# A spectral mixing and hard-swish kernel: the last four k of the first tokens computed straight from their spectrum, and two batches' stores moved between queues

## The chip, the cores and the metric

The kernel runs on one core of one Trainium2 chip. The metric is the device time of one execution, in microseconds (us), as the median of several runs. TensorE is called PE here, VectorE DVE, ScalarE ACT, GpSimd POOL and SyncE SP, as in the profile.

## The reference

The input x has 8 batches of 3008 tokens with 256 channels, in fp32. Each channel is filtered along the tokens by a real FFT, a product with a complex filter and an inverse FFT. Then every token passes through a two-layer network with a hard-swish.

```
X = np.fft.rfft(x, axis=1)
Y = X * (filt_r + 1j * filt_i)[None, :, :]
y = np.fft.irfft(Y, n=3008, axis=1)          # (8, 3008, 256)
h = y.reshape(24064, 256) @ w_in             # 256 -> 2048
g = h * np.clip(h + 3.0, 0.0, 6.0) / 6.0
out = g @ w_out                              # 2048 -> 256
```

## The kernel before, in words

**The transform.** 3008 is 47 times 64. Each batch passes five stages. Stage A multiplies by a 47-point table (`a_unit`, for batch 0 `a0_unit`, L302) and leaves 24 values of k with real and imaginary part. For batches 1 to 7 the result goes to DRAM (`z_store`, L342) and returns with k outside (`t2_load`, L350); for batch 0 it stays on chip and PE turns it (`turn`, L310). Stage B (`b_unit`, L355) multiplies each k by a 64-point table, which arrives together with that k's filter rows (`table_load`, L168, six pieces of four k). `f_unit` (L363) forms the filter products in three DVE operations for two k, and `y_unit` (L376) combines them in two more. `bi_unit` (L384) multiplies back and ACT copies the result to a tile t3 (two buffers). `g_store` (L396) writes t3 to DRAM, and `t4_load` (L415) reads it back with k on the partitions. Finally `n_unit` (L425) multiplies by the last table `wai` and writes chunks of up to five groups of 94 tokens into xn, the input of the network.

Batch 0 uses a shortcut: its `bi_unit` takes the raw products of `f_unit` (two tables `wi`), and `y_unit` is not run.

**The network.** Tokens go in blocks k of 512 (47 blocks) and the 2048 hidden units in eight parts p of 256. The main program from block 1 on is a seven-product scheme (`up_1` to `up_5`, `down`) software-pipelined by one part. Block 0 is computed in the plain form (`plain_up`, L536, and `plain_down`, L545), because the sums of the weights that the seven-product scheme needs are still being made. One pair (k, p) is called a step; block 0 is steps 0 to 7, and step 8 opens block 1.

**The weights.** The host passes 64-bit floats. DVE turns each of 16 pieces of 512 KB into fp32 (`w_conv`, L221, seven or eight operations a piece), from buffers `bits` that SP fills (`load_bits`, `w_load`). The letter string `W_AT` says which pool each piece's buffer is from: o (output tiles), g (hidden tiles) or x (tiles of the block sums xt). POOL then adds up the sums (`w_sums`, L249).

**The opening.** The program is written in order by hand under a manual schedule; each engine executes its instructions in that order. Everything ahead of step 0 is in L625 to L697: load batch 0's x into the space of the weights (`x0_load`, 32 transfers), `a0_unit` eight times with two `w_conv`, then a loop over the six table pieces c (L677) with two `b_unit` and `f_unit`, the `turn` for c+1, and `bi_unit` and `g_store` for the pair before. `t4_load` for the first 564 tokens (chunks 0 and 1) is called three times: for k 0 to 15, 16 to 19 and 20 to 23, each when its store has been issued. Then PE multiplies zeros nine times (`keep_warm(9)`), DVE converts three pieces (`convert(3, False)`), and `n_unit` is run for chunks 0 and 1 before step 0.

**The plan.** From step 0 on, `at(step, function)` puts the work of the other batches between the steps. In step s, functions listed in EARLY (matmul stages) come after the first products, the others at the end. Batch 1 has its eight `a_unit` in steps 2 to 9, each followed by `z_store`, its `t2_load` from step 10, and its `b_unit` from step 12.

**Queues.** SP issues nearly all loads and the output stores. In the opening ACT issues batch 0's `g_store` and two of the last `t4_load`; later POOL issues every `z_store` and `g_store`. A transfer's issue waits until the transfer eight places back has completed (in the instruction listing they rotate through eight completion counters); ACT and SP share one such set, and POOL has another.

```
for c in range(NT + 1):
    if c < NT:
        for i in (2 * c, 2 * c + 1):
            b_unit(0, i)
            f_unit(0, i)
    if c + 1 < NT:
        turn(c + 1)
    if c:
        bi_unit(0, 2 * c - 2)
        g_store(0, 2 * c - 2, nc.scalar)
```

Of the kernel before, what the change touches and what calls it, by code (L numbers as in the profile page):

```python
# [44 lines left out]
NBLK = B * N // BLK  # L45
NJ = 5
RING = 3 * BLK


def outer(j, h):  # L50
# [4 lines left out]
def _make_tables():  # L55
    a = np.arange(NA)
    c = np.arange(NC)
    wa = np.zeros((P, P))
    wai = np.zeros((P, HC, TOK))
    start = np.zeros((P, 2 * P))  # L60
    for h in range(2):
        for k in range(KH):
            th = 2 * np.pi * ((a * k) % NA) / NA
            for g in range(2):
                wa[h * 64:h * 64 + NA, g * 64 + k] = np.cos(th)
                wa[h * 64:h * 64 + NA, g * 64 + 32 + k] = -np.sin(th)
            start[h * 64:h * 64 + NA, P + 4 * k + h] = np.cos(th)
            start[h * 64:h * 64 + NA, P + 4 * k + 2 + h] = -np.sin(th)
    wb = np.zeros((P, KH, P))
    wi = np.zeros((P, 3, NC))  # L70
    re, im = slice(0, NC), slice(NC, P)
    for k in range(KH):
        for q in range(64):
            f, sign = (k + NA * q, 1.0) if q < 32 else (NA * (q - 31) - k, -1.0)
            th = 2 * np.pi * ((c * f) % N) / N
            cs, sn = np.cos(th), np.sin(th)
            if f in (0, NF - 1):
                sn = np.zeros(NC)
            wb[re, k, q], wb[im, k, q] = cs, sign * sn
            wb[re, k, HALF + q], wb[im, k, HALF + q] = -sn, sign * cs  # L80

    for q in range(64):
        g, sign = (q, 1.0) if q < 32 else (31 - q, -1.0)
        co, si = (f([2 * np.pi * ((j * g) % NC) / NC for j in range(HC + 1)]) for f in (np.cos, np.sin))
        ab = np.concatenate([co, np.zeros(HC - 1) if q == 63 else si[1:HC]])
        wi[q, 0], wi[HALF + q, 0] = ab, sign * ab
        wi[q, 1], wi[HALF + q, 1] = ab, -ab
        wi[q, 2], wi[HALF + q, 2] = sign * ab, sign * ab
    start[:, :P] = np.eye(P)
    for j in range(HC):  # L90
        for h in range(2):
            to = slice(h * NA, (h + 1) * NA)
            for k in range(KH):
                m = 2.0 if k else 1.0
                th = 2 * np.pi * ((a * k * NC + outer(j, h) * k) % N) / N
                cs, sn = m * np.cos(th), m * np.sin(th)
                s = -1.0 if h else 1.0
                if j:
                    wai[k, j, to], wai[32 + k, j, to] = cs, -sn
                    wai[64 + k, j, to], wai[96 + k, j, to] = -s * sn, -s * cs  # L100
                else:
                    wai[h * 64 + k, j, to], wai[h * 64 + 32 + k, j, to] = cs, -sn
    f = np.float32
    return wa.astype(f), (wai / N).astype(f), wb.astype(f), wi.astype(f), start.astype(f)


@with_exitstack
def kernel(
# [8 lines left out]
):  # L117
    nc = tc.nc

    wa_np, wai_np, wb_np, wi_np, start_np = _make_tables()  # L120
    wa_d = nc.inline_tensor(wa_np, name="wa_t").ap()
    wai_d = nc.inline_tensor(wai_np, name="wai_t").ap()
    wb_d = nc.inline_tensor(wb_np, name="wb_t").ap()
    wi_d = nc.inline_tensor(wi_np, name="wi_t").ap()
    start_d = nc.inline_tensor(start_np, name="start_t").ap()


    z_d = nc.dram_tensor("z_tmp", (B, KH, P, D), FP32, kind="Internal").ap()
    g_d = nc.dram_tensor("g_tmp", (B, NU, 2, 2, NC, D), FP32, kind="Internal").ap()

    def pool(name, bufs, **kw):
# [67 lines left out]

    W_AT = "ooggxxooxxooxxoo"

    def w_before(i):
        same = [j for j in range(i) if W_AT[j] == W_AT[i]]
# [1 line left out]

    def w_load(i, q):
        if W_AT[i] == "g":
            t = gp.tile([P, 7, 256], FP32, name="g").bitcast(I32)[:, 0:4, :].rearrange("p a n -> p (a n)")  # L210
        elif W_AT[i] == "x":
            t = xtp.tile([P, 4, 256], FP32, name="xt").bitcast(I32).rearrange("p a n -> p (a n)")
        else:
            t = op.tile([P, 1024], I32, name="bits", tag="o")
        q.dma_start(t.rearrange("p (a d) -> p a d", a=2), w_part(i)[0])
        st["bits", i] = t
# [122 lines left out]
            nc.scalar.activation(out=t[:, h, :, :].rearrange("p j d -> p (j d)"), in_=ps[h], func=AXT.Copy)  # L339
        st["t1", b, c] = t  # L340

    def z_store(b, c):  # L342
        t = st.pop(("t1", b, c))
        for g in range(2):
            for ri in range(2):
                p0 = g * 64 + ri * 32
                z = z_d[b, :, ts(ri, NC), :].rearrange("k (h j) d -> k h j d", h=2)
                nc.gpsimd.dma_start(z[:, :, ds(c * XC + 2 * g, 2), :], t[p0:p0 + KH, :, :, :])  # L348

    def t2_load(b, c):  # L350
        t = t2p.tile([P, TC, D], FP32, name="t2")
# [23 lines left out]

    def y_unit(b, i):  # L376
        s1, s2 = st["y", b, i]
        y = yp.tile([P, 2, D], FP32, name="y")
        nc.vector.tensor_tensor(out=y[0:HALF], in0=s1[0:HALF], in1=s1[HALF:P], op=ALU.subtract)
        nc.vector.tensor_tensor(out=y[HALF:P], in0=s2[0:HALF], in1=s2[HALF:P], op=ALU.add)  # L380
        st["y", b, i] = y


    def bi_unit(b, i):  # L384
        ys = [st.pop(("y", b, i + v)) for v in range(2)]
        ps = [psF.tile([P, 2, D], FP32, name="psf", tag="f") for ri in range(2)]
        for v, ri in ((0, 0), (1, 0), (0, 1), (1, 1)):

            w, y = (wi[ts(ri, 64), 0, :], ys[v][ts(ri, 64)]) if b else (wi[:, 1 + ri, :], ys[v][ri])
            nc.tensor.matmul(ps[ri][ts(v, 64)], w, y, start=True, stop=True)  # L390
        t = t3p.tile([P, 2, 2, D], FP32, name="t3")
        for ri in range(2):
            nc.scalar.activation(out=t[:, ri, :, :], in_=ps[ri], func=AXT.Copy)  # L393
        st["t3", b, i] = t

    def g_store(b, i, q=nc.gpsimd):  # L396
        t = st.pop(("t3", b, i))
        for v in range(2):
            q.dma_start(g_d[b, i + v].rearrange("ri u c d -> c (ri u) d"), t[ts(v, 64)].rearrange("p ri u d -> p (ri u) d"))

# [9 lines left out]
        b, j, n = chunks[i]  # L412
        return b * N + j * TOK, n * TOK

    def t4_load(i, k0=0, k1=KH, qs=None, more=0):  # L415
        b, j, n = chunks[i]
        n += more
        for h in range(2):
            for ri in range(2):
                p0 = h * 64 + ri * 32  # L420
                (qs or (nc.sync, nc.sync))[ri].dma_start(t4[p0 + k0:p0 + k1, ds(i % 2 * NJ, n), :].rearrange("k j d -> k (j d)"),
                                  g_d[b, k0 // 2:k1 // 2, ri, :, ds(h * HC + j, n), :].rearrange("i u j d -> i u (j d)"))


    def n_unit(i, dh):  # L425
# [9 lines left out]
            done += m  # L435
        if dh and (t + n) // BLK > t // BLK > 0:
            t_sums(t // BLK)

    def xb(k, d):
        return xn[:, d, ts(k % 3, BLK)]  # L440
# [178 lines left out]
    with tc.manual_schedule():  # L619

        st["start"] = p14p.tile([P, 2, 2, P], FP32, name="p14").rearrange("p a u m -> p (a u m)")
        nc.scalar.dma_start(st["start"][:, 0:2 * P], start_d)  # L625
        zero = rp.tile([P, 512], FP32, name="r", tag="r")
        nc.vector.memset(zero, 0.0)
        nc.vector.memset(top_c, -0x40000000)
        nc.vector.memset(half_c, 0.5)
        nc.vector.memset(x0[32:64, 0:8, :], 0.0)  # L630
        nc.gpsimd.memset(x0[32:64, 8:16, :], 0.0)
        nc.gpsimd.memset(x0[32:64, 16:HC, :], 0.0)
        loaded = done = 0

        def load_bits(most):
# [10 lines left out]
                done += 1  # L646
                load_bits(NCONV if act else 0)

        def keep_warm(n):
            ps = psU.tile([P, 512], FP32, name="al")  # L650
            for i in range(n):
                nc.tensor.matmul(ps, zero[:, P:2 * P], zero, start=True, stop=True)

        nc.scalar.activation(out=zero[:, 0:1], in_=half_c, func=AXT.Copy)
        nc.scalar.dma_start(wi, wi_d)
        keep_warm(2)
        for j in range(0, HC, 4):
            x0_load(j, 4)
            load_bits({4: 1, 12: 2}.get(j, 0))
        for c in range(FB):  # L660
            table_load(0, c)
        load_bits(3)
        for j in range(0, HC, 4):
            a0_unit(j)
            convert(j in (4, 12), False)
        nc.gpsimd.memset(t4, 0.0)
        for c in range(FB, NT):
            table_load(0, c)
            if c == 3:
                load_bits(4)  # L670
        load_bits(5)
        nc.sync.dma_start(wai[:, 0:8, :], wai_d[:, 0:8, :])
        load_bits(8)
        nc.sync.dma_start(wa, wa_d)
        for i in range(2):
            w_sums(i, False)
        turn(0)  # L677
        for c in range(NT + 1):
            if c < NT:
                for i in (2 * c, 2 * c + 1):  # L680
                    b_unit(0, i)
                    f_unit(0, i)
            if c + 1 < NT:
                turn(c + 1)
            if c:
                bi_unit(0, 2 * c - 2)
                g_store(0, 2 * c - 2, nc.scalar)
            if c > 3:
                t4_load(0, (0, KH - 2 * TC, KH - TC)[c - 4], (KH - 2 * TC, KH - TC, KH)[c - 4], (nc.sync, nc.scalar)
                        if c == NT else None, 1)  # L690
        keep_warm(9)
        convert(3, False)
        for i in range(2):
            for dh in range(2):
                n_unit(i, dh)
        for i in range(2, done):
            w_sums(i, False)  # L697

# [47 lines left out]
        for n in range(1, B):  # L746
            a_at, b_at, bi_at = places(n)
            for c, s in enumerate(a_at):
                at(s, a_unit, n, c)
                at(s, z_store, n, c)  # L750
                if c >= 3:
                    at(max(a_at[c - 3], s - 6), x_load, n, c)
                elif n > 1:
# [113 lines left out]
```

## Time and profile before

| what | value |
|---|---|
| median of 3 runs | 2749.97 us (2749.27 to 2754.78) |
| profiled execution: its own time | 2751.82 us |
| profiled execution: span | 2750.0 us |
| mean granted PE clock | 0.994 |
| PE busy | 2703.0 us, 98% of the span |
| DVE busy | 1948.8 us, 71% |
| ACT busy | 1327.2 us, 48% |
| POOL busy | 398.8 us, 15% |
| moved by DMA | 194.72 MB, 71 GB/s in the mean |

The profile is of one execution, on the core's own time axis from the span's start. A row of the groups or of the timeline names the line of the code, the engine, the operation, the tiles, and in brackets what ended the idle time before it. A table by stage gives for each stretch its length, then busy time of PE, PEld (weight loads), DVE, ACT and POOL with instruction counts, the granted PE clock (1.00 is full speed), the busy share of the DMA engines and their GB/s. An fp32 matmul shows as two records, so "x4" is two instructions.

### The profile page before, as it was taken

What the parts mean: (1) busy time and instruction counts of PE and PEld (TensorE: products, weight loads), DVE (VectorE), ACT (ScalarE), POOL (GpSimd) and SP (SyncE); (2) the same over time, 40 slices, a digit from 0 to 9 for tenths busy, and PEclk for the clock granted to TensorE, in tenths of its full rate; (3) what the DMA queues carried; (4) which work ended last, traced back from release to release, by engine and by line L of the source; (5) the groups of instructions that cost most, each with busy time, mean ns of one, the idle gap of its engine ahead of it and who ended that gap; (6) DMA issues with size and microseconds to landing.
All of it is one profiled execution on the core that took longest, in us unless ns stands there. A gap on an engine that the chain in (4) does not pass through costs nothing.

```text
span 2750.0 us, 47026 instructions
## 1 busy us (share of the span) xinstructions
PE 2703.0 (98%) x18086; PEld 2404.5 (87%) x18086; DVE 1948.8 (71%) x3407; ACT 1327.2 (48%) x2658; POOL 398.8 (15%) x616
## 2 busy tenths in 40 slices
PE   8899999999999999999999999999999999999997
PEld 5477888998889988999889998899988999999997
DVE  7767856777667775678756787577775777766665
ACT  3344455444554455444554445544445444545443
POOL 1341021100211012100121001210112100100000
PEclk9899999999999999999999999999999999999999
DMA  8533233221332213321233212332123321100000
GB/s 236 154 108 89 55 89 88 67 63 41 89 90 71 58 46 88 90 73 50 54 87 94 65 48 62 87 99 69 38 57 91 92 72 38 43 23 24 19 9 16
DMA packets 119180, 194.72 MB, mean 71 GB/s; under 512 B 21981, under 2 KB 83293, under 8 KB 118829
## 3 DMA queue, kind: packets, MB, share of 16 engines
q1 hardware_dynamic: 97383, 143.89, 18.2%
q0 software_dynamic: 17728, 44.23, 7.1%
q10 hardware_dynamic: 3846, 3.60, 0.5%
q8 instruction: 143, 2.34, 0.4%
q14 instruction: 80, 0.66, 0.1%
HBM read 119.80 MB, written 71.83 MB: 70 GB/s over the span
## 4 chain that ended last, share of the span: by engine, by line
PE 94%; DVE 2%; DMA 1%; POOL 1%; issue 1%; ACT 0%; SPq 0%; POOLq 0%; DVEq 0%; ACTq 0%
PE po L529 42%; PE al L453 23%; PE be L453 17%; PE psn L428 4%; PE psf L359 3%; PE psf L336 2%; PE psf L390 2%; POOL w_all L252 0%; PE po L305 0%; PE po L359 0%; DMA xs<-in_x_dram 0%; DMA t<-g_tmp 0%; DVE g L503 0%; PE po L551 0%; POOL z_tmp L348 0%
## 5 line engine op out<-in xcount | busy, mean ns | idle before, releaser
L529 PEld LDWEIGHTS po<-w_all,g 128*128 128x128 f32 x10304 | 1368.0, 191 | 144.4 <-issue 39.2
L529 PE MATMUL po<-w_all,g 128*128 128x128 f32 x10304 | 1398.7, 276 | 5.1 <-DVE g L503 4.4
L503 DVE SCALAR_TENSOR_TENSOR g<-r,h 128x512 f32<-128x512 f32 x736 | 506.7, 688 | 270.2 <-ACT r L498 257.6
L498 ACT ACTIVATE r<-h,half_c 128x512 f32<-128x512 f32 x736 | 531.2, 722 | 331.0 <-DVE h L479 319.0
L453 PE MATMUL al<-xt,w_all 128*128 128x256 f32 x2208 | 660.1, 381 | 4.1 <-ACT s L474 2.5
L479 DVE TENSOR_TENSOR h<-be,s 128x512 f32<-128x512 f32 x368 | 254.3, 691 | 263.8 <-PE be L453 251.3
L453 PE MATMUL be<-xn,w_all 128*128 128x256 f32 x1472 | 437.8, 379 | 0.0
L453 PEld LDWEIGHTS al<-xt,w_all 128*128 128x128 f32 x2208 | 335.3, 192 | 6.1 <-issue 3.7
L453 PEld LDWEIGHTS be<-xn,w_all 128*128 128x128 f32 x1472 | 279.7, 190 | 37.9
L493 ACT ACTIVATE h<-al 128x256 f32<-128x256 f32 x368 | 141.3, 384 | 348.2 <-PE al L453 348.2
L484 DVE TENSOR_TENSOR h<-al,s 128x256 f32<-128x256 f32 x368 | 156.3, 425 | 165.0 <-PE al L453 163.5
L511 DVE TENSOR_TENSOR g<-g 128x512 f32<-128x512 f32 x368 | 255.1, 693 | 12.6
L474 ACT ACTIVATE s<-al 128x256 f32<-128x256 f32 x368 | 141.5, 384 | 199.8 <-PE al L453 199.8
L465 ACT ACTIVATE s<-be 128x256 f32<-128x256 f32 x368 | 141.3, 384 | 176.1 <-PE be L453 176.1
L453 PE MATMUL al<-xn,w_all 128*128 128x256 f32 x736 | 219.9, 381 | 0.5 <-ACT h L493 0.5
L453 PE MATMUL be<-xt,w_all 128*128 128x256 f32 x736 | 218.9, 379 | 0.0
L348 POOL DMA_DIRECT2D z_tmp<-t x224 | 130.1, 584 | 418.8 <-ACT t L339 415.9
L464 ACT ACTIVATE s<-al 128x256 f32<-128x256 f32 x368 | 141.4, 384 | 68.0 <-PE al L453 67.9
L513 DVE TENSOR_TENSOR g<-g 128x256 f32<-128x256 f32 x368 | 160.6, 436 | 12.5
L510 DVE TENSOR_TENSOR g<-g 128x256 f32<-128x256 f32 x368 | 156.8, 426 | 12.6
L453 PEld LDWEIGHTS be<-xt,w_all 128*128 128x128 f32 x736 | 139.8, 190 | 18.9
L585 POOL TENSOR_TENSOR o<-p,o 128x256 f32<-128x256 f32 x45 | 32.6, 726 | 813.4 <-ACT t L393 392.7
(117 smaller groups left out, 1869.9 us busy)
## 6 DMA issues: line engine op xcount, KB each, us to landing
t<-g_tmp SPq DMA_DIRECT2D x188, 120.0 KB
z_tmp<-t POOLq DMA_DIRECT2D x224, 96.0 KB, 3.3
t<-z_tmp SPq DMA_DIRECT2D x42, 512.0 KB
g_tmp<-t POOLq DMA_DIRECT2D x84, 256.0 KB, 3.8
out_dram<-o SPq DMA_DIRECT2D x321, 47.0 KB
xs<-in_x_dram SPq DMA_DIRECT2D x112, 128.0 KB
ft<-in_filt_r_dram SPq DMA_DIRECT2D x88, 128.0 KB
ft<-in_filt_i_dram SPq DMA_DIRECT2D x88, 128.0 KB
```

Source lines behind the costliest of these rows:

```text
L453: nc.tensor.matmul(ps, w_in[p][:, w, :], x, start=start, stop=stop, skip_group_check=True)
L464: nc.scalar.activation(out=s[:, 0, :], in_=al, func=AXT.Copy)
L465: nc.scalar.activation(out=s5, in_=be[:, 1, :], func=AXT.Copy)
L474: nc.scalar.activation(out=s[:, 1, :], in_=al, func=AXT.Copy)
L479: nc.vector.tensor_tensor(out=st["h"][0].rearrange("p (a n) -> p a n", a=2), in0=be, in1=s, op=ALU.add)
L484: nc.vector.tensor_tensor(out=st["h"][1][:, 256:512], in0=al, in1=s5, op=ALU.add)
L498: nc.scalar.activation(out=r, in_=st["h"][i], func=AXT.Relu, bias=half_c, scale=1.0 / 6.0)
L503: nc.vector.scalar_tensor_tensor(out=st["g", k, p][:, o:o + 2, :].rearrange("p a n -> p (a n)"), in0=st["r", i], scalar=1.0, in1=st["h"][i ...
L510: v.tensor_tensor(out=g[:, G1, :], in0=g[:, G3, :], in1=g[:, G22, :], op=ALU.add)
L511: v.tensor_tensor(out=g[:, G3:G2 + 1:2, :], in0=g[:, G3:G1 + 1, :], in1=g[:, G11:G11 + 1, :].broadcast_to([P, 2, 256]), op=ALU.subtract)
L513: v.tensor_tensor(out=g[:, G4, :], in0=g[:, G12, :], in1=g[:, G2, :], op=ALU.subtract)
L529: nc.tensor.matmul(st["po", k][bank][:, part, u, :], g[:, a, ts(u, P)], w_out[p][:, w, :], start=(p == 0 and n in OPENS and u == 0), stop= ...
```

## The change

In short: for batch 0 and the first 564 tokens, k 20 to 23 no longer go through `bi_unit`, DRAM, `t4_load` and `n_unit`. `y_unit` now forms the combined spectrum of units 10 and 11 (two k each), and a new function `direct` multiplies it with a new table `direct_t` (128 x 4 x 564 fp32) straight to tokens. Its sums stay in four PSUM tiles, and `n_first` adds the products of k 0 to 19 on top and copies to xn. `bi_unit(0, 10)` and its `g_store` still run, after `n_first`, for the later chunks. Batch 0's stores g leave from POOL's queue in place of ACT's, in a new DRAM layout (`g0_d`) with runs of 2 KB in place of 1 KB on the DRAM side; its `t4_load` reads that layout in runs of 1 KB. Batch 1's `z_store` go out from SP in place of POOL. `keep_warm(9)` is gone. The loads of weight pieces 2 to 7 move behind the table loads. The x loads become five calls (20 transfers) in place of eight (32), and their memsets are cut smaller, the first ones ahead of the others. `W_AT` has o in place of x for pieces 12 and 13.

```
-    W_AT = "ooggxxooxxooxxoo"
+    W_AT = "ooggxxooxxoooooo"
...
-    def z_store(b, c):
+    def z_store(b, c, q=nc.gpsimd):
...
+    def direct(i):
+        if "psn" not in st:
+            st["psn"] = {(c, dh): (psO.tile([P, 2, 2, P], FP32, name="po%d" % (2 + dh)).rearrange("p a u m -> p (a u m)")
+                                   if c else psF.tile([P, 512], FP32, name="psn", tag="f"))
+                         for c in range(2) for dh in range(2)}
+        for u in range(2):
+            k = 2 * i + u - KH + TC
+            for (c, dh), ps in st["psn"].items():
+                t, n = token(c)
+                nc.tensor.matmul(ps[:, 0:n], st["y", 0, i][:, u, ts(dh, P)], st["direct"][k][:, ds(t, n)],
+                                 start=k == 0, stop=False, skip_group_check=True)
+
+    def n_first():
+        for (c, dh), ps in st.pop("psn").items():
+            b, j, n = chunks[c]
+            for q in range(n):
+                nc.tensor.matmul(ps[:, ts(q, TOK)], t4[:, j + q, ts(dh, P)], wai[:, j + q, :],
+                                 start=False, stop=True, skip_group_check=True)
+            nc.scalar.activation(out=xn[:, dh, ds(j * TOK, n * TOK)], in_=ps[:, 0:n * TOK], func=AXT.Copy)
...
+        nc.vector.memset(x0[32:64, 0:4, :], 0.0)
+        nc.gpsimd.memset(x0[32:64, 4:8, :], 0.0)
         nc.vector.memset(zero, 0.0)
...
-        nc.vector.memset(x0[32:64, 0:8, :], 0.0)
...
-        for j in range(0, HC, 4):
-            x0_load(j, 4)
-            load_bits({4: 1, 12: 2}.get(j, 0))
+        for j, n, bits in (0, 4, 0), (4, 4, 1), (8, 8, 2), (16, 8, 0), (24, 8, 0):
+            x0_load(j, n)
+            load_bits(bits)
         for c in range(FB):
             table_load(0, c)
-        load_bits(3)
...
+        for i in range(2):
+            w_sums(i, False)
         for c in range(FB, NT):
             table_load(0, c)
-            if c == 3:
-                load_bits(4)
-        load_bits(5)
+        last = x0_at(HC * D - 2048, 3 * ND)
+        nc.sync.dma_start(last, direct_d[:, 0:3, :].rearrange("p k n -> p (k n)"))
+        load_bits(3)
+        st["direct"] = [last[:, ts(k, ND)] for k in range(3)] + [st["rest"][:, 0:ND]]
+        nc.sync.dma_start(st["direct"][3], direct_d[:, 3, :])
         nc.sync.dma_start(wai[:, 0:8, :], wai_d[:, 0:8, :])
-        load_bits(8)
-        nc.sync.dma_start(wa, wa_d)
-        for i in range(2):
-            w_sums(i, False)
+        load_bits(4)
         turn(0)
-        for c in range(NT + 1):
-            if c < NT:
-                for i in (2 * c, 2 * c + 1):
-                    b_unit(0, i)
-                    f_unit(0, i)
+        for c in range(NT):
+            for i in (2 * c, 2 * c + 1):
+                b_unit(0, i)
+                f_unit(0, i)
+                if c == NT - 1:
+                    y_unit(0, i)
             if c + 1 < NT:
                 turn(c + 1)
             if c:
                 bi_unit(0, 2 * c - 2)
-                g_store(0, 2 * c - 2, nc.scalar)
+                g_store(0, 2 * c - 2)
             if c > 3:
-                t4_load(0, (0, KH - 2 * TC, KH - TC)[c - 4], (KH - 2 * TC, KH - TC, KH)[c - 4], (nc.sync, nc.scalar)
-                        if c == NT else None, 1)
-        keep_warm(9)
+                t4_load(0, (0, KH - 2 * TC)[c - 4], (KH - 2 * TC, KH - TC)[c - 4], 1)
+            if c == 4:
+                load_bits(5)
+        direct(NU - 2)
+        direct(NU - 1)
+        load_bits(8)
+        nc.sync.dma_start(wa, wa_d)
+        n_first()
+        bi_unit(0, NU - 2)
+        g_store(0, NU - 2)
         convert(3, False)
-        for i in range(2):
-            for dh in range(2):
-                n_unit(i, dh)
...
-                at(s, z_store, n, c)
+                at(s, z_store, n, c, nc.sync if n == 1 else nc.gpsimd)
```

## The prediction

> **What bounds the kernel now.** I read the page first. PE is busy 98% of the span and carries the chain that ended last, so after the opening the kernel is a fixed string of matmuls: what the opening loses or gains is carried to the end unless something behind it waits.
>
> ```profile
> span 2750.0 us, 47026 instructions
> PE 94%; DVE 2%; DMA 1%; POOL 1%; issue 1%; ACT 0%; SPq 0%; POOLq 0%; DVEq 0%; ACTq 0%
> ```
>
> Next the table by stage over the first 105 us (length, busy time of PE, PEld, DVE, ACT, POOL, then clock, DMA share, GB/s).
>
> ```profile
> 46.00:56.00 10.00, 7.31 (x29) 4.95 (x30) 4.70 (x7) 2.54 (x5) 0.00 (x0) 0.83 0.96 295
> 61.50:69.50 8.00, 8.00 (x19) 3.34 (x18) 7.76 (x15) 1.08 (x2) 1.87 (x3) 1.00 0.61 170
> 69.50:77.00 7.50, 0.04 (x1) 0.02 (x1) 4.83 (x9) 0.00 (x0) 3.22 (x6) 0.74 0.17 50
> 77.00:88.00 11.00, 10.76 (x32) 7.48 (x33) 0.69 (x1) 2.20 (x5) 0.00 (x0) 0.56 0.21 65
> ```
>
> From 61.5 to 77.0 PE does nothing useful (8 us of zeros, then idle), and to 88 it runs at 0.56 clock. The chain between 55 and 90 us and the waits say why: a store goes to DRAM, k 20 to 23 come back, the tables follow.
>
> ```profile
> 70.53 3.62 DMA t<-g_tmp
> 74.63 2.40 DMA xs<-in_x_dram
> 77.03 4.55 PE psn L428 x20
> 82.96 3.47 PE al L540 x4
> ...
> 89.11 0.69 DVE g L503
> ```
>
> Last, SP's own waits from 30 to 60 us, and the places behind the opening where PE or SP wait.
>
> ```profile
> SPq L215 <- DMA g_tmp<-t: 4.6, 1, 4.6
> SPq L178 <- DMA g_tmp<-t: 2.0, 1, 2.0
> ```
> ```profile
> 99.27 2.73 PE L540 MATMUL al<-xn,w_all 128*128 128x512 f32 x4 [3.98 <-DVE g L503]
> 162.86 15.03 SPq L606 DMA_DIRECT2D out_dram<-o  x14
> 178.23 2.98 SPq L352 DMA_DIRECT2D t<-z_tmp  x3
> ```
> ```profile
> ACT t L339 <- DMA z_tmp<-t: 8.2, 3, 3.7
> PE al L453 <- ACT s L474: 2.5, 1, 2.5
> ```
>
> SP stood 6.6 us behind batch 0's stores, whose completion counters it shares with ACT, so the tables for k 16 to 23 came late.
>
> **The change, step by step.** My yardstick is the end of block 0's first DVE pair (L503): 89.80 us now (89.11 + 0.69). From there DVE converts two pieces and releases PE at 99.27, 9.5 us later, whatever came before.
>
> *x loads and memsets.* The third x transfer waits for a DVE memset that ends at 3.67 (1.91 + 1.76). The new one is half as long and comes first: ready at 0.92 + 0.9 = 1.8. Twelve of SP's issues go (8.56 us for 16 at L290, 0.53 each), but the bytes stay and the DMA share is near 1.0 from 8 to 26 us; the larger second chunk also leaves PE idle again (it waited 2.50 us at 13.49). Bounds on the end of the 47-point stage (26.15): 0 to 3 us earlier; I take 1.0.
>
> *Tables.* Stores on POOL no longer stand before SP's issues, and 1 MB of weight pieces moves behind the tables. DVE's waits at L371 (3.74 us for the filter rows, 1.67 behind them) go. Late next is PE: L359 comes at 36.22 and 40.85, a period of 4.65. The last pair is then at 36.2 + 3 x 4.65 = 50.2, less 1.0 is 49.2 (55.01 now). DVE starts 1.2 later, as now (56.23 - 55.01). Units 10 and 11 take 2 x 2.14, and the new `y_unit` four operations of 64x512 at 0.687 (L379): 50.4 + 4.3 + 2.75 = 57.5 (60.5 now). So the added DVE work costs 2.75 us and is paid.
>
> *direct.* 16 matmuls of two sizes. 470 columns: the 512-column pair of L540 takes 3.48 us for four (88.19 to 91.67), 0.87 each, so 0.80; eight make 6.4. 94 columns: L428 warm takes 1.09 us for five (123.14), 0.22; eight make 1.7. Half of the 8.1 us lies under unit 11's DVE work; the other half follows 57.5 or the first half (which needs a PSUM tile that unit 11's product frees at 56.1): end about 62.6. Its tables, 1.16 MB, lie behind the filter tables on SP, 4 us at the 295 GB/s of 46 to 56; with the tables through by about 45 they are in by 52. If that cover were gone, each us late is a us lost.
>
> *Round trip of k 16 to 19, now the last.* `bi_unit(8)`: 51.2 to 53.1 (1.94 at L390); ACT copies to 53.7; two stores on POOL, 0.65 each, to 55.0. Landing: 3.0 to 7.4 us, median 3.8 (L399): 58.8. Four loads at 0.78 (3.91 for five): 62.0. Before, the last was issued by 72.6 and PE was released at 77.0, 4.5 later; a nearer landing would be 2. I take 65.0, bounds 64 and 68.
>
> *n_first and step 0.* 12 matmuls at 0.22 (warm) are 2.6, `bi_unit(10)` 1.9 with ACT's copies beside it: PE starts step 0 at 69.6 (82.75 now). Then 4 x 0.87, ACT 0.69, DVE 0.69: 74.5. DVE's three conversions take 13.95 (60.52 to 74.47), now from 57.5 to 71.5; plus 1.4 gives 72.9, so PE's path is later, by 1.6 us. Yardstick: 74.5 against 89.8, **15.3 us gained**.
>
> *Weight pieces, POOL's sums.* Pieces 4 to 7 arrive by about 68, needed from 67 (piece 4, issued near 58) to 80. Pieces 12 and 13 wait for conversions two back; about one conversion (4.5 us) is left for 512 KB, 2 us at 250 GB/s. Cost nothing; without this cover at most 2 us each. Behind PE's L540 wait there is the same 4 us gap, so the half clock after it (0.63 in 100.0 to 104.6) stays.
>
> *Batch 1's z_store on SP.* 32 issues at 0.55 are 18 us on SP, 19 less on POOL (0.58 each). POOL was late behind its sums, ACT stood 8.2 us behind its stores, and PE lost 2.5 (L453): that goes. On SP each store waits for ACT, and the x loads queue behind it; an x piece is issued three steps of 8 us ahead, so I charge nothing there. But the last eight stores now stand between the 14 output stores (15.0 us) and `t2_load`: 4.4 us of issue and 2.7 of landing, where `t2_load` had been issued at 178.23 and was needed at 188.15. Loads of 512 KB need about 4 more: slack of 6 shrinks by 7.1 and by the 2.5: a wait of 1 to 4; I take 1.5. Net here +1.0.
>
> *keep_warm, and two rules.* Removing the zeros: PE was idle 7.5 us after them and ran at 0.56. The Trainium skill (TensorE: Matmul & The Clock Gate, Part 1) says that an idle window of about 3.4 us halves the clock. My gaps before step 0 are at most 2.4 us, so warm; were they above, `n_first` and step 0 double, an estimate of about +6 us. Against moving stores to POOL speaks the skill's SBUF — State Buffer, section SBUF: two separate sides: fast DVE operations lock POOL out of writing descriptors, 620 ns becoming 3100. The row: POOL's `z_store` between conversions takes 0.58 to 0.79 and L399 0.63 to 0.67. By the rule the two critical stores cost 5 us more, by the row nothing; the operations there (products from PSUM, `y_unit`) are not the fast kind, so I go by the row.
>
> **The sum.** 15.3 + 1.0 is 16.3: span 2750.0 - 16.3 = 2733.7. The profiled execution took 2751.82, 1.85 above the median; from the median 2749.97, **2733.5 us**.
>
> **Rivals.**
> - *Late landing on POOL's queue* (10%): stores at 7.4 in place of 3.8, and t3's two buffers make `bi_unit` wait for a store two back. Round trip +3.6, one such wait +3: gain about 10, 2740. For it: DMA share near 1 until 56. Against: median 3.8 elsewhere.
> - *More at the front* (10%): x arrives in larger runs 2 us sooner than I take, the last loads land in 2, and DVE's conversions become the limit (72.9 less 2): gain about 21, 2728.
> - *The direct path doesn't shorten the wait* (5%): the tables or k 16 to 19 come as late as k 20 to 23 did, say 73, in a DMA queue still full. Step 0 then starts at 77.6: gain 5, 2745.
> - *SP becomes the bound in steps 2 to 12* (3%), slower: if the 18 us of stores found no gaps and each x load and `t2_load` came later by them, the stores and 1 us of waits for ACT would give 19 against 15: 2754. It decides once more than 16 us reach PE. Against: SP is idle 14 us before the outputs, 122 to 127 and elsewhere.
>
> **Chances.** The sum as it stands, 72%, 2728 to 2739. A measurement of this kernel can tell about 0.2% (5.5 us) from no change. Faster by more 0.92, within 0.05, slower 0.03. Range 2725 to 2742.
>
> **What would show it.** PE at full clock up to step 0, which starts near 70; no SP wait for g stores between 30 and 50; L371 without the 3.7 us wait; yardstick near 74.5; no wait of ACT for z stores; a short PE wait for `t2_load` near 172. Wrong if PE idles over 4 us before `n_first`, if x or `t2_load` waits exceed 5 us, or if DVE's conversions wait for weight pieces.

## The result, and the profile after

| | before | after |
|---|---|---|
| median of the runs, us | 2750.51 (2749.27 to 2754.78, 4 runs) | 2741.52 (2739.87 to 2742.31, 4 runs) |
| profiled execution: own time, span | 2751.82, 2750.0 | 2741.89, 2740.1 |

The ratio is 0.9964, with a 95% interval of 0.9947 to 0.9981. The change takes 9.0 us off; 16.5 were forecast. In the profiled executions it is 9.9 us of span, and all that follows is read from those.

First the page of the changed kernel, the span and the chain's shares:

```profile
span 2740.1 us, 47054 instructions
PE 95%; DVE 3%; DMA 1%; issue 0%; POOL 0%; ACT 0%; SPq 0%; POOLq 0%; DVEq 0%; ACTq 0%
```

PE's share was 94% and is 95%; the shares are whole per cents, and the new `y_unit` operations are not on the chain. Then the same four stages as before (length, busy time of PE, PEld, DVE, ACT, POOL, then clock, DMA share, GB/s):

```profile
46.00:56.00 10.00, 9.30 (x44) 4.78 (x40) 9.28 (x14) 4.45 (x8) 2.26 (x4) 1.00 0.86 283
61.50:69.50 8.00, 4.70 (x21) 3.28 (x20) 7.76 (x16) 0.00 (x0) 0.00 (x0) 0.89 0.93 240
69.50:77.00 7.50, 7.50 (x33) 5.23 (x33) 3.24 (x7) 2.60 (x6) 0.43 (x1) 0.67 0.65 165
77.00:88.00 11.00, 8.67 (x29) 4.82 (x27) 8.86 (x14) 4.51 (x7) 7.28 (x14) 1.00 0.35 96
```

The 7.5 us without PE and the 8 us of zeros are gone; from 46 to 56 PE works 9.3 us of 10, where it had 7.3. But the clock is 0.67 from 69.5 to 77.0, which the forecast had at full. The chain of waits in that stretch:

```profile
56.27 0.43 POOL g_tmp L413
56.69 0.10 issue
56.79 4.47 DMA g_tmp<-t
...
62.66 5.50 DMA xt<-in_moe_w_out_dram
68.17 0.08 issue
68.25 4.55 PE psn L477 x20
...
75.10 1.91 PE al L582 x4
...
79.49 0.69 DVE g L545
```

The store of k 16 to 19 lands at 61.26, four loads go out to 62.62, and PE gets on at 68.25. (The chain names the weight piece that was issued behind the loads; what to make of that is tested below.) `n_first`'s first ten products (x20) take 4.55 us, a time that the kernel before showed at half clock. The yardstick is at 79.49 + 0.69 = 80.18.

SP's own waits from 30 to 60 us, the two longest:

```profile
SPq L439 <- DMA g_tmp<-t: 14.4, 4, 10.7
SPq L187 <- DMA w_all<-wb_t: 1.9, 2, 0.9
```

L439 is `t4_load`, which needs what was stored. No table and no weight piece stands behind a store any more. Behind the opening:

```profile
90.24 3.78 PE L582 MATMUL al<-xn,w_all 128*128 128x512 f32 x4 [4.57 <-DVE g L545]
```
```profile
153.28 11.96 SPq L648 DMA_DIRECT2D out_dram<-o  x14
165.29 5.86 SPq L359 DMA_DIRECT2D z_tmp<-t  x8
173.43 1.49 SPq L363 DMA_DIRECT2D t<-z_tmp  x3
```
```profile
ACT t L350 <- DMA z_tmp<-t: 0.7, 1, 0.7
PE al L495 <- ACT s L516: 0.5, 1, 0.5
```

PE still waits for DVE ahead of step 2. The eight z stores stand where the forecast put them, between the outputs and `t2_load`, and PE has no wait for `t2_load` at all. ACT's waits for z stores fell from 8.2 to 0.7 us and PE's wait for ACT from 2.5 to 0.5.

### The profile page after: what moved, and what is told of

Same layout as the page of the kernel before. It is cut to its first block, busy times and chain, and to the rows that moved or that the text cites. A ratio compares the mean times of both kernels' runs of the same rounds, so it can differ in the third digit from the quotient of the medians.

```text
span 2740.1 us, 47054 instructions
## 1 busy us (share of the span) xinstructions
PE 2700.9 (99%) x18100; PEld 2405.9 (88%) x18100; DVE 1950.4 (71%) x3411; ACT 1325.8 (48%) x2658; POOL 385.6 (14%) x598
## 4 chain that ended last, share of the span: by engine, by line
PE 95%; DVE 3%; DMA 1%; issue 0%; POOL 0%; ACT 0%; SPq 0%; POOLq 0%; DVEq 0%; ACTq 0%
PE po L571 42%; PE al L495 23%; PE be L495 17%; PE psn L449 4%; PE psf L370 3%; PE psf L347 2%; PE psf L403 2%; PE po L593 1%; PE po L316 1%; PE po L370 0%; PE al L582 0%; DVE g L545 0%; PE be L582 0%; DMA w_all<-in_x_dram 0%; DMA xt<-in_moe_w_out_dram 0%
## 5 line engine op out<-in xcount | busy, mean ns | idle before, releaser
L540 ACT ACTIVATE r<-h,half_c 128x512 f32<-128x512 f32 x736 | 531.0, 721 | 329.4 <-DVE h L521 317.3
L553 DVE TENSOR_TENSOR g<-g 128x512 f32<-128x512 f32 x368 | 255.1, 693 | 12.6
L359 POOL DMA_DIRECT2D z_tmp<-t x192 | 110.7, 581 | 414.9 <-ACT t L350 412.5
```

Source lines behind the costliest of these rows:

```text
L540: nc.scalar.activation(out=r, in_=st["h"][i], func=AXT.Relu, bias=half_c, scale=1.0 / 6.0)
L553: v.tensor_tensor(out=g[:, G3:G2 + 1:2, :], in0=g[:, G3:G1 + 1, :], in1=g[:, G11:G11 + 1, :].broadcast_to([P, 2, 256]), op=ALU.subtract)
```

## The experiments

Twelve kernels were run. Each starts from the changed kernel unless it says otherwise. The first two columns after the name are times in the profiled execution, the next two are differences, which do not depend on how the front of that execution went. The kernel before was timed again beside each group of kernels (e1 to e4, e5 to e8, e9 to e11, e12); its medians there were 2752.37, 2752.06, 2750.43 and 2750.54 us. So a difference of under 2 us between medians of different groups shows nothing.

| kernel | 47-point stage ends | step 0 | step 2 less stage end | span less step 2 | span | median (runs) |
|---|---|---|---|---|---|---|
| before | 26.15 | 82.75 | 73.1 | 2650.7 | 2750.0 | 2750.51 (4) |
| after | 27.55 | 75.03 | 62.7 | 2649.9 | 2740.1 | 2741.52 (4) |
| e1_memset | 25.78 | 73.10 | 62.5 | 2649.6 | 2737.9 | 2740.49 (4) |
| e2_warm | 30.54 | 75.45 | 60.2 | 2648.5 | 2739.3 | 2741.14 (4) |
| e3_late | 25.78 | 73.16 | 63.1 | 2649.5 | 2738.4 | 2741.83 (5) |
| e4_no_direct | 27.31 | 76.20 | 65.9 | 2649.7 | 2742.9 | 2744.31 (6) |
| e5_pieces | 26.39 | 73.44 | 62.3 | 2650.0 | 2738.7 | 2741.43 (5) |
| e6_act_store | 26.11 | 80.85 | 70.1 | 2648.9 | 2745.1 | 2748.60 (20) |
| e7_z_pool | 26.37 | 73.77 | 63.1 | 2650.3 | 2739.8 | 2743.20 (7) |
| e8_conv4 | 26.85 | 73.95 | 58.4 | 2651.3 | 2736.5 | 2737.94 (4) |
| e9_conv4_warm | 26.28 | 71.60 | 57.9 | 2650.4 | 2734.6 | 2736.68 (5) |
| e10_hold | 26.34 | 71.97 | 61.3 | 2649.5 | 2737.1 | 2739.87 (4) |
| e11_before_pool | 25.37 | 76.21 | 67.5 | 2652.0 | 2744.8 | 2748.66 (20) |
| e12_bits_zpool | 27.46 | 74.39 | 62.7 | 2653.5 | 2743.6 | 2745.07 (12) |

The column "span less step 2" moves by 1 to 2 us, and by 3 in e12: most of what the opening gains or loses stays to the end, as the forecast assumed. My theory after the result was that the shortfall lies in three places, the front, the landing of k 16 to 19, and the clock behind PE's gap before `n_first`. The rivals were that the stores on POOL land late, and that the edit in steps 2 to 12 cost more than 1 us.

**e1_memset: do POOL's memsets hold the x loads up?**

```
-        nc.gpsimd.memset(x0[32:64, 8:16, :], 0.0)
+        nc.vector.memset(x0[32:64, 8:16, :], 0.0)
```

> The changed kernel with one memset of x0 moved: columns 8 to 15 are cleared by DVE in place of POOL, so that POOL's memsets end near 5.2 us in place of 6.9 and the third x transfer finds its rows cleared early. If POOL's four memsets hold the x transfers up (theory 1), PE is released from its first wait at about 11.9 instead of 13.58, the gap before it is under 2 us, the 47-point stage ends near 25.3 instead of 27.55, and the span falls by about 2 us. If the bytes of x and of the first weight pieces set that time (theory 2), PE is released at 13.4 to 13.7 as before, the stage ends within 0.4 us of 27.55, and the span stays within 1 us.

PE's row in the timeline at the end of that wait:

```profile
13.20 12.58 PE L316 MATMUL po<-p,w_all 111*128 111x128 f32 x96 [2.37 <-DMA w_all<-in_x_dram]
```

PE is released at 13.20, against 13.58 in the changed kernel and 13.14 in e3_late, whose memsets are those of the changed kernel. Theory 1, 11.9, is out, though the chain of the changed kernel had led through the four memsets. The stage did end 1.8 us sooner, but so it did in e3_late: with this front unedited the stage ended at 25.8 to 27.6 in ten executions (after, e3 to e10 and e12; mean 26.6), and with the old front at 26.15 and 25.37. The forecast's 1.0 us of gain there isn't in the rows; if anything the new front is about 0.9 later, which two executions of the old one can't settle. What spreads the ends is when the x pieces land and how long half clock lasts behind the gap before the second chunk: 3.4 us of it in e1 and e3, where the 96 records take 12.6 us, 6.8 us in the changed kernel and e4, where they take 14.0.

**e2_warm: what does the half clock cost?**

```
+            if j == 8:
+                keep_warm(2, zero[:, P:2 * P], zero)
             a0_unit(j)
...
         direct(NU - 1)
+        keep_warm(3, st["direct"][0][:, 0:P], st["direct"][0][:, 0:470])
```

> The changed kernel with matmuls on spare data put into two waits of PE: two of 512 columns in the wait near 10 to 13.6 us, three of 470 columns between the direct products and n_first. If the half clock after these gaps is what made the 47-point stage and n_first longer than forecast (theory 1), the 96 products of the stage take 12.7 us or less instead of 13.97 (end near 26.2), n_first's 24 products take 2.7 instead of 5.4, step 0 starts near 71 instead of 75.1, and the span falls by 3 to 4 us. If the clock falls anyhow (theory 2), the durations stay at 13.9 and 5.4 and the span stays within 1 us. If DVE's conversions, done at 72.8, and not PE then hold the next step (theory 3), step 0 starts near 71 but the end of the first DVE pair moves from 80.2 only to about 76, and PE's release at 90.2 with it.

The stretch from `n_first` to step 0, first in the changed kernel, then in e2_warm (columns as above):

```profile
68.25:75.10 6.85, 6.85 (x33) 5.54 (x33) 4.45 (x9) 1.51 (x4) 0.00 (x0) 0.54 0.78 208
```
```profile
71.35:75.45 4.10, 4.10 (x33) 3.12 (x33) 3.96 (x9) 1.52 (x5) 0.00 (x0) 1.00 1.06 279
```

The same 33 recorded matmuls take 4.10 us at clock 1.00 and 6.85 at 0.54, so theory 1 holds for this gap: 2.75 us of PE time went there. Step 2 started 60.2 us behind the stage end in place of 62.7, so the gain was not lost to DVE, and theory 3 is out. In the front the test failed: the x pieces came late in this execution (a second wait of 3.22 us, stage end 30.54), so nothing can be read there. The median, 2741.14, shows no gain that can be told from none.

**e3_late: are the weight pieces in the way of k 16 to 19?**

```
-        load_bits(8)
-        nc.sync.dma_start(wa, wa_d)
         n_first()
         bi_unit(0, NU - 2)
         g_store(0, NU - 2)
+        load_bits(8)
+        nc.sync.dma_start(wa, wa_d)
```

> The changed kernel with weight pieces 5 to 7 and the table wa issued after n_first in the order of the program, so that on SP nothing but piece 4 and the loads of k 16 to 19 stands behind k 0 to 15. If the three 512 KB pieces issued at 62.7 to 63.7 hold up the landing of k 16 to 19 (theory 1), PE's wait before n_first of 3.3 us falls to about 0.5 to 1 and n_first starts near 65.5. If k 16 to 19 need 4.5 to 5.5 us to come down whatever stands behind them (theory 2), n_first starts at 67.5 to 68.5 as before. In both cases the pieces themselves come later: if DVE's second or third conversion then waits for them, its end moves from 72.8 to 75 or more and eats a part.

This was a poor edit: nothing in these lines makes SP wait, so SP issues the same loads in the same order, 0.04 us behind the last load of k 16 to 19. It tests neither theory and is of use only as the changed kernel run once more: gap before `n_first` 3.74 us, `n_first` to step 0 6.2 us, median 2741.83.

**e5_pieces and e10_hold: the same question put rightly**, once with the four pieces ahead of everything, once with pieces 5 to 7 and what is behind them held until `n_first` has begun.

```
-        load_bits(4)
+        load_bits(8)
         turn(0)
```

> The changed kernel with weight pieces 4 to 7 (2 MB) issued on SP right behind piece 3, near 42 us, where SP otherwise stands from 42.3 to 57.0, so that no 512 KB load is left around the loads of k 0 to 19. If those pieces hold up the landing of k 16 to 19 (theory 1), n_first starts 2 to 3 us after SP's last load instead of 5.6, PE's gap before it falls from 3.3 us to under 1.5, the clock stays full, n_first's 24 products take near 3 us instead of 5.4, and step 0 starts about 5 us sooner after the end of the direct products (5 instead of 10.1); the span falls by 3 to 5. If k 16 to 19 take 5.3 to 6 us to come down in any case (theory 2), all of that stays and the span is within 1 us of 2740.

```
+        if i == 5:
+            nc.scalar.activation(out=t.bitcast(FP32)[:, 0:1], in_=xn[:, 0, 0:1], func=AXT.Copy)
         q.dma_start(t.rearrange("p (a d) -> p a d", a=2), w_part(i)[0])
```

> The changed kernel with the load of weight piece 5 made to wait for n_first's first copy (ACT writes one column of its tile, out of n_first's output, ahead of the load), so that pieces 5 to 7, the table wa and the x pieces of batch 1 stand still on SP until n_first has begun. If PE's wait for k 16 to 19 is lengthened by what is issued behind them (theory 1), n_first starts 2 to 3 us behind SP's last load of k 16 to 19 instead of 5.3 to 6, PE's gap falls under 1 us, and the 24 products take near 3 us. If the four loads of 24 KB take that long by themselves (theory 2), n_first starts 5 us or more behind the last load as before. The pieces then come 10 us later: conversions in step 0 or PE's first x products may wait, so that the span may be longer in both cases.

PE's row at the start of `n_first`, first e5_pieces, then e10_hold:

```profile
66.38 4.51 PE L477 MATMUL psn<-wai,t 128*128 128x94 f32 x20 [2.44 <-DMA xs<-in_x_dram]
```
```profile
66.52 2.89 PE L479 MATMUL psn<-wai,t 128*128 128x94 f32 x20 [2.76 <-DMA t<-g_tmp]
```

Counted from SP's last load of k 16 to 19, PE is released after 5.6 us in the changed kernel (5.3 to 6.2 in e1, e3, e7, e8 and e12, whose loads there are the same), 5.0 in e10_hold (61.53 to 66.52) and 3.7 in e5_pieces (62.69 to 66.38). So the pieces behind the loads cost 0.3 to 1.2, and the chain's "xt" was only the transfer that ended last in the same wait. Piece 4, issued just ahead, costs about 1.3, and 3.7 us are left for the four loads themselves; each of these two rests on one execution. Neither theory holds as it was put: the landing is mostly its own, and partly piece 4. Nor was it all gain: in e5_pieces the g stores landed in a median of 5.7 us in place of 4.5 while 2 MB moved beside them, SP got its loads out later, and `n_first` began 40.0 us behind the stage end in place of 40.7. In both kernels the clock halved behind gaps of only 2.44 and 2.76 us.

**e4_no_direct, e6_act_store, e11_before_pool: which part carries the gain?** In e4 k 20 to 23 go through DRAM again, with nine products of zeros; e6 puts batch 0's stores back on ACT's queue; e11 is the kernel before with only those stores on POOL.

```
-                nc.gpsimd.dma_start(g0_d
+                nc.scalar.dma_start(g0_d
```

> The changed kernel without the direct products: k 20 to 23 of block 0 go through DRAM as in the kernel before, with nine matmuls of zeros in the wait, and all four loads precede n_unit; front, queues, layout of the scratch tensor and the later z stores stay as changed. If the direct products carry most of the gain (theory 1), step 0 starts 5 to 7 us later than 75.1 and the span is 2744 to 2748. If the tables that come earlier carry it (theory 2), step 0 starts within 2 us of 75.1 and the span stays near 2741.

> The changed kernel with batch 0's g stores on ACT's queue, as in the kernel before, all else as changed. If SP's 6.6 us behind those stores came from their queue (theory 1), SP stands again behind g stores between 40 and 57 us, piece 3 or the loads of k 0 to 15 go out 2 to 5 us later, and step 0 starts later by 1 to 4. If the order of the tables had done it, since after the change all tables are issued before the stores land (theory 2), nothing is late on SP; ACT's queue may even land the two last stores sooner than the 4.5 us on POOL, and step 0 starts 0 to 2 us sooner after the end of the direct products.

> The kernel before with one edit: batch 0's g stores on POOL's queue in place of ACT's. If that queue alone carries most of the change's gain (theory 1), SP's 6.6 us behind g stores and PE's 3.1 us for a table at 48.7 go, k 20 to 23 come 5 to 7 us sooner, and the span is 2743 to 2746 against 2750. If the gain needs the new order of the tables and the direct products (theory 2), SP then waits for something else, the last stores land later on POOL, and the span is within 2 us of 2750.

SP's waits from 30 to 60 us in e6_act_store, and PE's row at the third table pair:

```profile
SPq L189 <- DMA g_tmp<-t: 7.2, 2, 6.6
...
SPq L711 <- DMA g_tmp<-t: 1.9, 1, 1.9
SPq L187 <- DMA g_tmp<-t: 1.8, 1, 1.8
```
```profile
48.77 3.43 PE L370 MATMUL po<-t,w_all 128*128 128x256 f32 x8 [3.35 <-DMA w_all<-wb_t]
```

SP's longest wait in the same stretch in e11_before_pool, and the start of step 0 in e4_no_direct:

```profile
SPq L421 <- DMA g_tmp<-t: 10.3, 4, 6.1
```
```profile
76.20 3.68 PE L582 MATMUL al<-xn,w_all 128*128 128x512 f32 x4
```

L187, L189 and L711 are loads of tables. With the stores on ACT they stand 10.9 us behind stores that they don't need (in the traces SP's and ACT's transfers take turns on the same eight semaphores, POOL's on eight others), and PE's wait for a table, 3.10 us before, is back. In e11 only L421 (`t4_load`) still stands behind stores, the ones that it reads. Behind the stage end, step 2 comes 7.4 us later than in the changed kernel without POOL's queue (e6), 3.2 later without the direct products (e4), and 5.6 sooner than before with POOL's queue alone (e11, 67.5 against 73.1). The 5.6 of the queue alone and the 3.2 that the direct products add make 8.8 of the 10.4 us; 1.6 is left for the other edits and what the parts do together. So theory 1 of e6 and of e11 holds in the rows, by more than was expected of e6, and the direct products are the smaller part: step 0 came only 1.2 us later without them, not 5 to 7, though step 2 lost 3.2, since step 0 began at half clock (its first four records took 3.68 us for 1.98).

These sums rest on one execution of each kernel. The timed runs, each set against the kernel before in its own group, gained 9.0 us (changed kernel), 8.1 (e4), 3.5 (e6) and 1.8 (e11: 2748.66, ratio 0.9992, 0.9985 to 0.9999). They agree that the change without POOL's queue loses most of its gain. They do not tell the 0.9 us of the direct products from none, and they do not confirm 5 us for the queue alone: e11's profiled execution, 2746.63, is 2.0 us below its median, and that of the kernel before, 2751.82, is 1.3 above 2750.51. So how the gain divides between the two edits is open.

**e7_z_pool and e12_bits_zpool: what took the waits near step 10 away?** e7 puts batch 1's z stores back on POOL; e12 also puts weight pieces 12 and 13 back in the buffers `xt`.

```
-                at(s, z_store, n, c, nc.sync if n == 1 else nc.gpsimd)
+                at(s, z_store, n, c)
```
```
-    W_AT = "ooggxxooxxoooooo"
+    W_AT = "ooggxxooxxooxxoo"
```

> The changed kernel with batch 1's z stores back on POOL's queue. If SP's queue for them is worth what the forecast put there or a little more (theory 1), PE waits again 2 to 2.5 us for ACT near step 10, ACT again 8 us for its own stores, and the span is 1.5 to 2.5 us longer, all of it between step 8 and step 14. If DVE bounds these steps (theory 2), the waits show but PE's step 12 starts at the same distance behind step 2 and the span is within 0.7 us of 2740.

> The changed kernel with batch 1's z stores back on POOL's queue and, besides, weight pieces 12 and 13 back in the buffers named xt, in which POOL also forms the sums of block 1 (t_sums). If it is the pieces' buffers, and not the queue of the z stores, that took ACT's 8.2 us of waits and PE's 2.5 us away (theory 1), POOL stands 8 to 12 us before t_sums near 120 us, ACT waits again 5 to 9 us for its own z stores, PE again 2 to 2.5 us for ACT near 140 to 150, and the span is 2 to 3 us above the 2739.8 of the kernel with the z stores alone on POOL, if its opening is alike. If the buffers are not the cause (theory 2), POOL's wait may show, but ACT's and PE's waits stay away and the distance from step 2's start to the end stays at 2650.

In e7 the waits stayed away (PE's wait for ACT 0.5 us, no wait of ACT for z stores), and the distance from step 2 to the end is 2650.3 against 2649.9. In e12 they came back; POOL's, PE's and ACT's rows:

```profile
122.43 1.17 POOL L488 TENSOR_TENSOR xt<-xn 128x256 f32<-128x256 f32 x1 [11.07 <-issue]
```
```profile
150.72 0.84 PE L495 MATMUL al<-xt,w_all 128*128 128x256 f32 x2 [2.54 <-ACT s L516]
```
```profile
ACT t L350 <- DMA z_tmp<-t: 4.5, 2, 2.7
```

The kernel before has the same row on POOL, which the forecast left out; ahead of it stands DVE's last read of a weight piece in `xt`:

```profile
130.71 0.69 DVE L240 SCALAR_TENSOR_TENSOR y<-xt,y 128x512 f32<-128x512 f32 x1
131.91 0.80 POOL L446 TENSOR_TENSOR xt<-xn 128x256 f32<-128x256 f32 x1 [11.28 <-issue]
```

So theory 1 of e12 holds, with ACT's 4.5 us a little under the 5 to 9 expected: with pieces 12 and 13 in `xt`, POOL stands 11 us at `t_sums` until such a buffer is free (DVE's last read of a piece there ends at 122.29 in e12, POOL goes on at 122.43; 131.40 and 131.91 in the kernel before), its z stores queue behind that, ACT waits for them and PE for ACT. The distance to the end is 2653.5, 3.2 us more than e7: PE's wait of 2.5, with 3.4 us of half clock behind it (151.1 to 154.5). So the new letters of `W_AT` for pieces 12 and 13, which I had priced at nothing, are enough to remove these waits, and neither theory of e7 held. Given them, no gain of SP's queue for the z stores is shown: e7 is 0.4 us longer from step 2 to the end and 1.7 in the median (2743.20 against 2741.52), but the medians are from different groups, and 140 us behind step 2 (ACT's L540) e7 is 1.4 us ahead of the changed kernel. Whether SP's queue alone would have removed them too, with the old buffers, was not tried.

**e8_conv4 and e9_conv4_warm: the 10 us behind the yardstick.** DVE is idle from 72.84 until ACT's output at 77.77, and up to the yardstick but for one operation; then it converts two pieces while PE waits.

```
-        convert(3, False)
+        convert(4, False)
...
-        for i, s in enumerate((0, 0, 1, 2, 2, 3, 4, 4, 5, 5, 6)):
+        for i, s in enumerate((0, 1, 2, 2, 3, 4, 4, 5, 5, 6)):
```

> The changed kernel with one more weight piece converted ahead of step 0 (four in place of three, and one less in step 0), in the 6.6 us in which DVE stands idle from 72.8 to 79.5. If after the first pair PE waits only for DVE's two conversions (theory 1), PE is released for step 2 at 5.5 to 6 us behind the end of that pair instead of 10.1, 4.5 us sooner, PE's gap before it is under 0.5 us and no half clock follows it (2 to 3 us more); of that 3 to 7 us stay in the span if the later steps have slack on DVE. If DVE stays the bound up to step 8 (theory 2), the release comes sooner but PE waits elsewhere up to 140 us and the span falls by 0 to 2 us.

> The changed kernel with both edits that moved PE so far: four weight pieces converted ahead of step 0, and three matmuls of 470 columns of spare data between the direct products and n_first. If the two gains add (theory 1), n_first's 24 products take near 3 us, step 0 starts about 7.7 us behind the end of the direct products, step 2 starts right behind step 1, and the span is 2 to 3 us below the 2736.5 of the four conversions alone, near 2734. If DVE, which now ends its fourth conversion only at about 77.3, takes the place of PE (theory 2), step 0 starts sooner but its first DVE pair waits, step 2 starts at most 0.5 us sooner than with the four conversions alone, and the span stays within 1 us of 2736.5.

 (e9 is e8 with the second `keep_warm` of e2.)

PE's row at the start of step 2 in e8, then at the start of step 1 in e9:

```profile
85.22 1.98 PE L582 MATMUL al<-xn,w_all 128*128 128x512 f32 x4
```
```profile
77.23 1.98 PE L582 MATMUL al<-xn,w_all 128*128 128x512 f32 x4 [1.93 <-DVE g L545]
```

In e8 PE goes on without a gap, at full clock, 4.3 us nearer to the stage end; 1.4 of that is given back (2651.3), of which a wait of 2.00 us for a z store at 100.11, and half clock behind it from 102.3 to 105.7, are the visible part. In e9 step 0 starts 1.8 us sooner relative to the stage end than in e8, but then waits 1.93 us for DVE, so that step 2 gains 0.4: theory 2 of e9. e9 has the lowest median, 2736.68, ratio to the kernel before 0.9949 (0.9936 to 0.9961), 4.8 us under the changed kernel, whose ratio is 0.9964 (0.9947 to 0.9981): the intervals overlap, though no execution of e9 is as slow as one of the changed kernel. It isn't told apart from e8 (2737.94).

## Why the forecast of the gain was too high

The sign and the path were right, the size was not: the forecast gain is 1.8 times the measured one. The 2741.52 lies outside the 2728 to 2739 that was given 72%, and inside the range, 2725 to 2742, by only 0.5 us, which is in part luck. (The forecast's own sum, 16.3 from 2749.97, makes 2733.7, not 2733.5.) By its own steps, in the profiled execution:

- *x loads and memsets*: 25.2 forecast, 27.55 measured, outside the bounds of 0 to 3 us of gain. **2.35 us**. Nothing arrived sooner: PE's release before the second chunk was at 13.58, 13.49 in the kernel before. And the 96 records took 13.96 us for 12.65, since half clock lasted 6.8 us behind that gap for 3.4 before; this 1.3 us differs from execution to execution.
- *Tables*: right to 0.1 us. The period is 4.66 (4.65 taken), `y_unit` of unit 11 ends 32.3 us behind the stage end (57.5 - 25.2 = 32.3), and the waits at L371 (now L382) are gone. Its cause, stores ahead of SP's issues, is shown by e6.
- *direct*: about 8.6 us with its gaps, forecast 8.1; its tables were in time.
- *Round trip*: `n_first` began 40.7 us behind the stage end, 39.8 forecast. **0.9 us**. The stores took 4.5 to land (3.8 taken), the loads' issue 1.3 (3.1 taken), the landing 5.6 (3.0 taken).
- *n_first and step 0*: 6.85 us, 4.6 forecast. **2.25 us**. This is the step that failed in kind: "at most 2.4 us, so warm". The gap was 3.3 us, and it was no matter of its length alone: 2.44 us in e5 was followed by half clock too. What it cost is shown by e2.
- Step 0 to the yardstick: 5.1 for 4.9, **0.2**. Behind it DVE took 10.06 for 9.47, **0.6**.
- *Batch 1's z stores*: net 1.0 forecast; step 2 to the end gained 0.8, **0.2**. The size is right by luck. The gain of 2.5 us comes without the queue edit, by the buffers (e7 and e12), and the wait of 1.5 for `t2_load` isn't there, since the outputs took 12.0 us and not 15.0 and `t2_load` was out at 173.43, early enough. But little of it stays: against it stand, among others, half clock behind step 2 (4.8 us for 3.4) and a wait of 0.95 us for DVE at 138, and counted from the start of step 2, ACT's rows (L540, L498 before) come 0.55 us sooner than before at 61 us and 0.02 sooner at 140. What reaches the end comes from elsewhere: 12.4 us pass behind the last matmul, 13.6 before.

The terms make 2.35 + 0.9 + 2.25 + 0.2 + 0.6 + 0.2 = 6.5, which with 9.9 is the 16.4 of the sum (16.3, rounded). Of the 6.5, 3.6 is half clock in the front and behind the gap before `n_first`.

Of the rivals, *late landing on POOL's queue* came near in its number (2740) and not in its mechanism: the stores landed in 2.9 to 7.9, median 4.5, and ACT waited 2.3 us for `t3`'s buffers, PE not at all (its 1.0 us ahead of the direct products was for ACT's copy out of PSUM). *More at the front* did not come: the stage ended later. SP did not become a bound. Of the two rules, the one against stores on POOL was rightly put aside: the twelve issues took 0.55 to 0.73 us, those of the critical pair too. Beside that pair DVE formed products from PSUM, so the rule itself isn't tested here.

The other was used as a threshold, and these traces show none. PE's rows of two gaps in e9_conv4_warm:

```profile
13.26 3.81 PE L316 MATMUL po<-p,w_all 111*128 111x128 f32 x32 [2.26 <-DMA w_all<-in_x_dram]
98.25 2.07 PE L347 MATMUL psf<-xs,wa 47*64 47x512 f32 x8 [1.24 <-DMA xs<-in_x_dram]
```

The first stayed at full clock, the second was followed by half clock from 100.3 to 103.7. Nor does the length of a gap set how long half clock lasts: 2.44 us in e5 brought 6.8 us of it, 3.35 us in e6 (at 48.77) 3.4, and 3.98 us ahead of step 2 brought 3.4 in the kernel before and 6.8 in e4. The same section of the Trainium skill (TensorE: Matmul & The Clock Gate, Part 1) says that the activity window of about 3.4 us runs freely, so that the moment of warming up depends on where in it the first matmul lands. If that holds for a gap as well, its place counts besides its length. What the traces show agrees: every spell of half clock in the first 110 us of the fourteen profiles lasts 3.4 us or two, three or four times that. No run here moves a gap alone against the window.

## What to carry to other kernels

Before pricing a queue edit, look at what the next bound is fed by: SP's issues were shortened, but the x bytes came no sooner. A gap of PE in the forecast needs a price even when it is short; here half clock cost 1.3 us in the front and 2.75 before `n_first`, and three products on spare data took the second back. And every edit of a change has to be followed to an idle row: the 11 us of POOL at `t_sums` stood in the profile of before, and the edit that looked like bookkeeping took them away.

## What was not expected of the hardware

- Half clock outlasts its gap by far: in the changed kernel, from about 13.0 to 19.9, 67.7 to 74.5 and 88.2 to 95.0 (granted clock), 6.8 us each, beside gaps of 3.5, 3.3 and 4.6 us. It begins anywhere from 2 us before PE resumes (the third) to 2 us after (e9_conv4_warm, behind 98.25).
- Four loads of 24 KB took 3.7 us from the last issue to PE's release with no 512 KB load close to them, and 5.0 to 6.2 with one or more.
- SP's issue of a z store took 0.37 us (median of 32), 0.58 on POOL; 0.55 had been taken for SP.
- The time of an execution goes with its mean granted clock. The 20 executions of e11 spread over 5.4 us: its six at 0.995 average 2747.3, its three at 0.992 2751.0. In the 25 of the kernel before beside them, five at 0.995 average 2749.3 and two at 0.992 2753.3. In e6 it hardly shows (2747.9 at 0.996, 2748.5 at 0.993). Why one execution has more half clock than another was not found.
